# Linear attention and a two-layer FFN on one core: the low part of a decoded weight chunk is subtracted on VectorE instead of GpSimd

## The chip, the cores and the metric

One core of a Trainium2 chip runs the whole program. The metric is device time in microseconds. The core has TensorE (PE) for matrix products, VectorE (DVE), ScalarE (ACT) and GpSimd (POOL) for elementwise work, and SyncE (SP), which issues the transfers here. Each engine runs its own list of instructions in order.

## The reference

Eight batches, eight heads, 576 positions, 64 values a head. Linear attention with a normed output feeds a low-rank mixing over positions and a two-layer FFN of width 512 to 2048 to 512:

```python
kv = np.einsum('bhsd,bhse->bhde', k, v)
out = np.einsum('bhsd,bhde->bhse', q, kv)
rms = np.sqrt(np.mean(out * out, axis=-1, keepdims=True) + 1e-06)
x = out / rms * g_norm            # then heads side by side: [8, 576, 512]
...
h = x.transpose(0, 2, 1) @ U @ V
u = x + h.transpose(0, 2, 1)
ch = np.maximum(u @ w_ch1, 0.0) @ w_ch2
return (u + ch)
```

U, V and the two FFN weights arrive as 64-bit floating-point numbers, so the kernel receives their bits as 64-bit words and has to decode them itself.

## The kernel before

**Two parts for each number.** A product of full precision is made of three products of a shorter type (F32R): every operand is split into a high part, rounded by ScalarE, and a low part, the difference to it. FFN1 is thus high x high, high x low and low x high (lines 372 to 374), and FFN2 the same (line 389).

**The FFN.** The 4608 rows of u are cut into nine blocks of 512. For each block j, a loop runs over the 16 chunks f of the hidden width, 128 wide. `ffn1` makes 12 products into the one PSUM bank h (`ps_h`, one buffer). `relu` reads that bank twice: ScalarE writes the high part hh (line 381), then VectorE the low part hl (line 382); after that the bank can be filled again. `ffn2` adds the chunk before to four accumulators y, 12 products more. At the end of a block `finish` adds u in two steps, one on VectorE (line 400) and one on GpSimd (line 401), and writes the block out.

**The weights.** All 16 chunks stay in SBUF once they are decoded. Chunk 0 is decoded in the startup by a path of its own. Chunks 1 to 15 are decoded inside block 0, at most two chunks ahead (`AHEAD`) of the loop. One chunk is 128 partitions x 1024 words, w1 and w2 side by side. `decode_w` takes these steps:

- ScalarE's abs of the upper 32-bit half (line 82) into a temporary `dec`, of which there are two buffers;
- four VectorE operations on `dec`: clamp (line 85), shift and mask (86), merge the sign (88), merge the low bits (90);
- `split`: ScalarE copies `dec` into the high part (line 95), then an engine that is passed in subtracts it from `dec` and writes the low part (line 96). The buffer of `dec` is free after that.

The raw chunk and the finished one share their place in SBUF (`weight_slot`).

**The attention work.** While block j runs, the attention of batch j+1 is done in small steps between the FFN's: for each of four pairs of heads, the kv product (line 219), the output product (240, 242), its norm (243 to 267, of which 253 is a sum over 640 values and 255 to 258 are tiny operations on 128x10), a transposition (293) with 32 small transfers into `ut` (296), a split (103, 115, 281), the product with U (304, 313) and with V (364, 366), and the split of u (329, 330). In block 0 these steps stand closer together than later (`STEPS0`). In the startup the same work is done for batch 0 by lines 290 to 357, with line 348 as the split of u.

**What sets the order.** The program text gives a rough order, by the table `PLAN` in the startup and by the numbers of `STEPS0` and `STEPS` later. From that a scheduler lays out each engine's list when the kernel is built, by its own costs of the operations; so the lists move when an operation goes from one engine to another.

Of the kernel before, what the change touches and what calls it, by code (L numbers as in the profile page):

```python
# [47 lines left out]
def build(ctx: ExitStack, tc: tile.TileContext, kv_in, kvt0_in, kvt_in, q_in, uv_in, g_in, w_in, out):  # L48
    nc = tc.nc
# [22 lines left out]
    def weight_slot(name, shape, dtype, f):  # L72

        return const.tile(shape, dtype, name=name, tag=f"w_{f}")

    def decode(raw, tmp, n=None):

        words = raw.bitcast(U32).rearrange("p (n t) -> p n t", t=2)
        low, high = words[:, :, 0], words[:, :, 1]
        bits = tmp.bitcast(U32)  # L80
        if n is None or ENG["ab"][n] == "a":
            nc.scalar.activation(out=tmp, in_=high.bitcast(F32), func=AF.Abs)
        else:
            nc.vector.tensor_scalar(out=bits, in0=high, scalar1=0x7fffffff, scalar2=None, op0=ALU.bitwise_and)
        nc.vector.tensor_scalar(out=tmp, in0=tmp, scalar1=ABS_LO, scalar2=ABS_HI, op0=ALU.max, op1=ALU.min)  # L85
        nc.vector.tensor_scalar(out=bits, in0=bits, scalar1=3, scalar2=0x3fffffff,  # L86
                                op0=ALU.logical_shift_left, op1=ALU.bitwise_and)
        nc.vector.scalar_tensor_tensor(out=bits, in0=high, scalar=0xC0000000, in1=bits,  # L88
                                       op0=ALU.bitwise_and, op1=ALU.bitwise_or)
        nc.vector.scalar_tensor_tensor(out=bits, in0=low, scalar=29, in1=bits,  # L90
                                       op0=ALU.logical_shift_right, op1=ALU.bitwise_or)

    def split(hi, lo, src, lo_eng):

        nc.scalar.copy(out=hi, in_=src)  # L95
        lo_eng.tensor_tensor(out=lo, in0=src, in1=hi.bitcast(F32), op=ALU.subtract)  # L96
# [72 lines left out]
    def keep(which, f, hi, lo):  # L169
        w_sb[which][f] = [t.rearrange("p (d c) -> p d c", c=P) for t in (hi, lo)]  # L170
# [8 lines left out]
    def decode_w(f):  # L179

        tmp = dec.tile([P, 2 * DM], F32, name="dec")
        decode(raws.pop(f).rearrange("p w c -> p (w c)"), tmp)
        w = weight_slot(f"ws{f}", [P, 2, 2, DM], F32R, f)
        t = tmp.rearrange("p (w c) -> p w c", w=2)
        split(w[:, 0], w[:, 1], t, nc.gpsimd)
        for n, which in enumerate(("w1", "w2")):
            keep(which, f, w[:, 0, n], w[:, 1, n])

# [336 lines left out]
    for j in range(NBLK):  # L525
        todo = prep_schedule(j + 1)
        y = None
        for f in range(NF):
            if j == 0:
                while ahead < min(NF, f + 1 + AHEAD):  # L530
                    decode_w(ahead)
                    ahead += 1
            end = False
            if j == 0 and f < NEARLY:
                h = hs[f]
                ffn1(h, f, [3], j)
            else:
                end = j == NBLK - 1 and f == NF - 1
                h = ps_p.tile([P, BLK], F32, name="pp") if end else ps_h.tile([P, BLK], F32, name="h")
                ffn1(h, f, range(ND), j)  # L540
            hcur = (f, *relu(h, end))
            for w in todo.get(2 * f, []):
                w()
            if hprev is not None and not (j == NBLK - 1 and f > NF - 3):
                ffn2(y_prev if f == 0 else y, [hprev])
            if f == 0:
                if j > 0:
                    finish(y_prev, j - 1)
                y = outputs(j)
            for w in todo.get(2 * f + 1, []):  # L550
                w()
            held = (held + [hcur])[-3:]
            hprev = hcur
        y_prev = y
# [58 lines left out]
```

## Time and profile before

| | |
|---|---|
| time, median of 3 runs | 941.3 us (940.36 to 941.7) |
| the profiled execution | 941.2 us, span 939.4 us |
| mean granted TensorE clock | 0.993 of full speed |
| TensorE busy | 913.4 us, 97% of the span, 4550 products |
| VectorE busy | 428.2 us, 46%, 824 instructions |
| ScalarE busy | 237.6 us, 25% |
| GpSimd busy | 88.7 us, 9% |
| of it the 15 subtractions of line 96 on 128x1024 | 37.4 us, mean 2495 ns |

A row of a group gives line, engine, operation, the tile written and the tiles read, partitions x columns and type, the count, the busy time and the mean length. L96 is line 96 of the kernel. "PE h L372 <- DVE hl L382: 6.1, 4, 2.4" says that the TensorE product of line 372 into h waited 6.1 us in all, four times, at most 2.4 us, for the VectorE instruction of line 382 that wrote hl. In a timeline a row starts with its start and length in microseconds, counted from the start of the span; a bracket at its end is the idle time of the engine ahead of it, and what ended it. An instruction counts as busy from its start to its end, so time in which it stands inside is busy time too. The granted clock is 1.00 at full speed.

### The profile page before, as it was taken

What the parts mean: (1) busy time and instruction counts of PE and PEld (TensorE: products, weight loads), DVE (VectorE), ACT (ScalarE), POOL (GpSimd) and SP (SyncE); (2) the same over time, 40 slices, a digit from 0 to 9 for tenths busy, and PEclk for the clock granted to TensorE, in tenths of its full rate; (3) what the DMA queues carried; (4) which work ended last, traced back from release to release, by engine and by line L of the source; (5) the groups of instructions that cost most, each with busy time, mean ns of one, the idle gap of its engine ahead of it and who ended that gap; (6) DMA issues with size and microseconds to landing.
All of it is one profiled execution on the core that took longest, in us unless ns stands there. A gap on an engine that the chain in (4) does not pass through costs nothing.

```text
span 939.4 us, 11992 instructions
## 1 busy us (share of the span) xinstructions
PE 913.4 (97%) x4550; PEld 763.3 (81%) x4550; DVE 428.2 (46%) x824; ACT 237.6 (25%) x483; POOL 88.7 (9%) x82
## 2 busy tenths in 40 slices
PE   8789899999999999999999999999999999999998
PEld 7667678888888888888888888888788888888887
DVE  6999996445454344353354345334333331112112
ACT  5554442322222222222122222222222221111110
POOL 2333330100020002000110002000200020002000
PEclk9899999999999999999999999999999999999999
DMA  9951121321222112121122122212111010001001
GB/s 339 407 215 48 34 58 57 99 67 56 62 89 82 33 57 82 47 66 55 35 74 80 30 73 69 80 33 69 60 52 26 13 46 1 0 1 46 1 1 45
DMA packets 45034, 65.48 MB, mean 70 GB/s; under 512 B 9904, under 2 KB 28080, under 8 KB 44976
## 3 DMA queue, kind: packets, MB, share of 16 engines
q1 hardware_dynamic: 44976, 64.71, 21.2%
q8 instruction: 36, 0.59, 0.3%
q14 instruction: 22, 0.18, 0.1%
HBM read 46.97 MB, written 9.44 MB: 60 GB/s over the span
## 4 chain that ended last, share of the span: by engine, by line
PE 84%; DVE 13%; DMA 1%; issue 1%; SPq 0%; ACT 0%; POOL 0%; DVEq 0%; POOLq 0%
PE y L389 37%; PE h L372 13%; PE h L373 13%; PE h L374 13%; DVE dec L88 3%; PE pp L219 2%; PE pp L240 2%; DVE dec L90 2%; DVE dec L86 2%; PE pp L304 2%; DVE dec L85 1%; DVE hl L382 1%; DMA w1raw<-w_in 1%; PE pp L364 1%; PE pp L389 1%
## 5 line engine op out<-in xcount | busy, mean ns | idle before, releaser
L389 PE MATMUL y<-hh,ws 128*128 128x512 f32 (+1 forms) x1072 | 351.0, 394 | 0.1
L382 DVE SCALAR_TENSOR_TENSOR hl<-h,hh 128x512 fp32r<-128x512 f32 x142 | 97.8, 689 | 307.8 <-ACT hh L381 307.2
L389 PEld LDWEIGHTS y<-hh,ws 128*128 128x128 f32 x1072 | 194.3, 188 | 36.0 <-ACT hh L381 0.8
L372 PE MATMUL h<-uth,ws 128*128 128x512 f32 x536 | 212.5, 397 | 6.9 <-DVE hl L382 6.9
L373 PE MATMUL h<-utl,ws 128*128 128x512 f32 x536 | 210.1, 392 | 0.0
L374 PE MATMUL h<-uth,ws 128*128 128x512 f32 x536 | 209.9, 392 | 0.0
L389 PE MATMUL y<-hl,ws 128*128 128x512 f32 (+1 forms) x536 | 207.6, 387 | 0.0
L381 ACT ACTIVATE hh<-h 128x512 fp32r<-128x512 f32 x142 | 84.8, 597 | 409.2 <-PE h L374 409.1
L372 PEld LDWEIGHTS h<-uth,ws 128*128 128x128 f32 x536 | 101.4, 189 | 31.0 <-DVE hl L382 10.8
L374 PEld LDWEIGHTS h<-uth,ws 128*128 128x128 f32 x536 | 101.2, 189 | 21.9
L373 PEld LDWEIGHTS h<-utl,ws 128*128 128x128 f32 x536 | 101.4, 189 | 20.4
L389 PEld LDWEIGHTS y<-hl,ws 128*128 128x128 f32 x536 | 100.6, 188 | 20.5
L401 POOL TENSOR_TENSOR st<-st,utl 128x512 f32<-128x512 f32 x32 | 40.7, 1296 | 676.7 <-DVE st L400 673.6
L366 DVE TENSOR_TENSOR ut<-pp,ut 128x288 f32<-128x288 f32 x56 | 25.0, 456 | 53.6 <-DMA ut<-xt 39.0
L96 POOL TENSOR_TENSOR ws<-dec,ws 128x1024 fp32r<-128x1024 f32 x15 | 37.4, 2495 | 60.6 <-ACT ws L95 60.6
L400 DVE TENSOR_TENSOR st<-y,uth 128x512 f32<-128x512 f32 x32 | 21.2, 686 | 44.5 <-PE y L389 33.0
L329 ACT ACTIVATE uth<-ut,g_sb 128x448 fp32r<-128x448 f32 (+7 forms) x56 | 27.6, 530 | 48.0 <-DVE ut L366 33.6
L330 DVE SCALAR_TENSOR_TENSOR utl<-ut,g_sb,uth 128x448 fp32r<-128x448 f32 (+7 forms) x56 | 28.2, 534 | 14.7 <-ACT uth L329 10.9
L253 DVE TENSOR_REDUCE ss<-x 128x10 f32<-128x640 f32 x32 | 26.1, 814 | 19.0 <-ACT x L244 19.0
L219 PE MATMUL pp<-kv_sb 128*128 128x128 f32 x232 | 31.4, 275 | 0.5 <-DVE t L313 0.5
L219 PEld LDWEIGHTS pp<-kv_sb 128*128 128x128 f32 x232 | 29.3, 191 | 2.0 <-DVE t L313 0.9
L240 PE MATMUL pp<-kvb,q_sb 128*128 128x128 f32 x224 | 29.6, 274 | 0.0
(192 smaller groups left out, 754.8 us busy)
## 6 DMA issues: line engine op xcount, KB each, us to landing
raw<-w_in SPq DMA_DIRECT2D x30, 512.0 KB, 10.2
kv_sb<-kv_in SPq DMA_DIRECT2D x29, 512.0 KB, 3.5
q_sb<-q_in SPq DMA_DIRECT2D x29, 288.0 KB, 2.9
out<-st SPq DMA_DIRECT2D x32, 256.0 KB, 2.0
ut<-xt SPq DMA_DIRECT2D x224, 20.0 KB, 1.8
ut<-xt SPq DMA_DIRECT2D x224, 16.0 KB, 1.8
kvt_sb<-kvt_in SPq DMA_DIRECT2D x27, 128.0 KB, 3.2
kvq<-kv_in SPq DMA_DIRECT2D x3, 512.0 KB, 7.7
```

The source lines that it names most:

```text
L88: nc.vector.scalar_tensor_tensor(out=bits, in0=high, scalar=0xC0000000, in1=bits, op0=ALU.bitwise_and, op1=ALU.bitwise_or)
L96: lo_eng.tensor_tensor(out=lo, in0=src, in1=hi.bitcast(F32), op=ALU.subtract)
L219: nc.tensor.matmul(pp[:, 0:P], lhsT=m[:, i * P:(i + 1) * P], rhs=m[:, MAIN + i * P:MAIN + (i + 1) * P], start=(i == 0 and b < NATIVE), sto ...
L240: nc.tensor.matmul(big[:, i * P:(i + 1) * P], lhsT=qt[:, TAIL + i * P:TAIL + (i + 1) * P], rhs=kb, start=True, stop=True)
L330: nc.vector.scalar_tensor_tensor(out=lo, in0=src, scalar=g_sb, in1=hi.bitcast(F32), op0=ALU.mult, op1=ALU.subtract)
L372: nc.tensor.matmul(h, lhsT=w1s[f][0][:, d, :], rhs=uh[:, d, :], start=(d == 0), stop=False)
L373: nc.tensor.matmul(h, lhsT=w1s[f][0][:, d, :], rhs=ul[:, d, :], start=False, stop=False)
L374: nc.tensor.matmul(h, lhsT=w1s[f][1][:, d, :], rhs=uh[:, d, :], start=False, stop=(d == ND - 1))
L381: nc.scalar.activation(out=hh, in_=h, func=AF.Relu)
L382: nc.vector.scalar_tensor_tensor(out=hl, in0=h, scalar=0.0, in1=hh.bitcast(F32), op0=ALU.max, op1=ALU.subtract)
L389: nc.tensor.matmul(acc, lhsT=w2s[f][w][:, c, :], rhs=h[:, cols], start=(f == 0 and w == 0 and h is hh), stop=(f == NF - 1 and w == 1))
L401: nc.gpsimd.tensor_tensor(out=o, in0=o, in1=ul[:, c, :].bitcast(F32), op=ALU.add)
```

## The change

In `decode_w`, VectorE is passed to `split` instead of GpSimd:

```diff
         t = tmp.rearrange("p (w c) -> p w c", w=2)
-        split(w[:, 0], w[:, 1], t, nc.gpsimd)
+        split(w[:, 0], w[:, 1], t, nc.vector)
         for n, which in enumerate(("w1", "w2")):
```

`split` itself stays as it is. Fifteen instructions of line 96 go from GpSimd's list to VectorE's, and the lists of the other engines are laid out anew.

The first place is VectorE's list at the end of the startup, up to the first two low parts of the relu (hl, line 382). raw_151 and raw_162 are the raw words of the first two chunks decoded here, ws_515 and ws_524 the same chunks finished; raw_166 and raw_177 are the next two. Before:

```order
L90 SCALAR_TENSOR_TENSOR dec<-raw_162,dec 128x1024
L348 SCALAR_TENSOR_TENSOR utl<-y,g_sb,uth 128x512
L85 TENSOR_SCALAR dec<-dec 128x1024
L348 SCALAR_TENSOR_TENSOR utl<-pp,g_sb,uth 128x512
L86 TENSOR_SCALAR dec<-dec 128x1024
L88 SCALAR_TENSOR_TENSOR dec<-raw_166,dec 128x1024
L85 TENSOR_SCALAR dec<-dec 128x1024
L90 SCALAR_TENSOR_TENSOR dec<-raw_166,dec 128x1024
L86 TENSOR_SCALAR dec<-dec 128x1024
L382 SCALAR_TENSOR_TENSOR hl<-pp,hh 128x512
L382 SCALAR_TENSOR_TENSOR hl<-h,hh 128x512
```

The same place after the change:

```order
L90 SCALAR_TENSOR_TENSOR dec<-raw_162,dec 128x1024
L96 TENSOR_TENSOR ws_515<-dec,ws_515 128x1024
L348 SCALAR_TENSOR_TENSOR utl<-y,g_sb,uth 128x512
L96 TENSOR_TENSOR ws_524<-dec,ws_524 128x1024
L348 SCALAR_TENSOR_TENSOR utl<-pp,g_sb,uth 128x512
L85 TENSOR_SCALAR dec<-dec 128x1024 x2
L86 TENSOR_SCALAR dec<-dec 128x1024 x2
L88 SCALAR_TENSOR_TENSOR dec<-raw_166,dec 128x1024
L88 SCALAR_TENSOR_TENSOR dec<-raw_177,dec 128x1024
L382 SCALAR_TENSOR_TENSOR hl<-pp,hh 128x512
L382 SCALAR_TENSOR_TENSOR hl<-h,hh 128x512
```

Two subtractions have come in ahead of the second and the third L348, and the next two chunks go side by side through lines 85, 86 and 88 ahead of the first hl.

The second place is VectorE's list between the low part of the relu of the fourth chunk and that of the fifth (f = 3 and 4). Before:

```order
L382 SCALAR_TENSOR_TENSOR hl<-h,hh 128x512
L88 SCALAR_TENSOR_TENSOR dec<-raw_183,dec 128x1024
L90 SCALAR_TENSOR_TENSOR dec<-raw_183,dec 128x1024
L85 TENSOR_SCALAR dec<-dec 128x1024
L86 TENSOR_SCALAR dec<-dec 128x1024
L88 SCALAR_TENSOR_TENSOR dec<-raw_186,dec 128x1024
L382 SCALAR_TENSOR_TENSOR hl<-h,hh 128x512
```

The same place after the change, where ws_742 and ws_804 are the chunks of raw_180 and raw_183:

```order
L382 SCALAR_TENSOR_TENSOR hl<-h,hh 128x512
L96 TENSOR_TENSOR ws_742<-dec,ws_742 128x1024
L90 SCALAR_TENSOR_TENSOR dec<-raw_183,dec 128x1024
L85 TENSOR_SCALAR dec<-dec 128x1024
L86 TENSOR_SCALAR dec<-dec 128x1024
L96 TENSOR_TENSOR ws_804<-dec,ws_804 128x1024
L88 SCALAR_TENSOR_TENSOR dec<-raw_186,dec 128x1024
L382 SCALAR_TENSOR_TENSOR hl<-h,hh 128x512
```

Two subtractions have come in, and the L88 of raw_183 has moved ahead of the first hl. In GpSimd's list the 15 rows of line 96 on 128x1024 are gone, the four on 128x64 have stayed.

## The prediction

> **What bounds the kernel now.** The page comes first. Its 40 slices are 23.5 us each; VectorE (DVE) is full in slices 2 to 6 and less than half busy later, and the granted TensorE clock reads 9 or more from the third slice on.
>
> ```profile
> span 939.4 us, 11992 instructions
> ...
> DVE  6999996445454344353354345334333331112112
> ...
> PEclk9899999999999999999999999999999999999999
> ```
>
> Busy time by stretch, for core 0, says where the kernel is short of VectorE. The stretches from 53 to 141 us belong to the first FFN block, in which the weight chunks are decoded; the last one is the steady state behind it.
>
> ```profile
> core 0: us, PE busy (x) PEld busy (x) DVE busy (x) ACT busy (x) POOL busy (x), PEclk, DMA share, GB/s
> ...
> 53.00:70.00 17.00, 14.56 (x58) 11.58 (x57) 16.96 (x21) 7.80 (x9) 7.39 (x3) 0.90 0.40 153
> ...
> 84.00:100.00 16.00, 15.47 (x81) 12.41 (x81) 15.77 (x16) 8.16 (x14) 4.79 (x2) 1.00 0.20 60
> 100.00:120.00 20.00, 15.79 (x71) 11.98 (x69) 19.90 (x25) 8.85 (x14) 7.49 (x3) 0.91 0.18 46
> 120.00:141.00 21.00, 20.36 (x103) 16.65 (x104) 19.35 (x24) 8.89 (x15) 7.63 (x3) 1.00 0.21 60
> 141.00:200.00 59.00, 59.00 (x307) 49.82 (x306) 32.23 (x77) 16.95 (x39) 5.17 (x4) 1.00 0.26 80
> ```
>
> Up to 141 us VectorE has no free time (16.96 of 17 us, 19.90 of 20 us) and TensorE has gaps; from 141 us on TensorE is full (59.00 of 59 us) and VectorE is about half busy. So only time taken out of VectorE before 141 us can shorten the run, and only as far as TensorE stands still there. How far that is, TensorE's own waits in 38 to 142 us say (engine and line, what it waited for, total, times, longest); these are the four largest:
>
> ```profile
> PE h L372 <- DVE hl L382: 6.1, 4, 2.4
> PE pp L304 <- DVE xh L281: 1.7, 1, 1.7
> PE y L389 <- DVE hl L382: 1.2, 1, 1.2
> PE pp L242 <- DVE x L265: 1.1, 1, 1.1
> ```
>
> All are waits for VectorE, 10.1 us together. The next FFN1 product (L372) cannot start until hl (L382), the low half of the relu, has read the only h bank. After a wait the granted clock is down too: 0.90 over 17 us and 0.91 over 20 us, 1.7 + 1.8 = 3.5 us of TensorE time. These 10.1 + 3.5 = 13.6 us are about all that can be won.
>
> **What the moved instruction costs where it is.** GpSimd's (POOL) and VectorE's timelines, laid beside each other (start us, us, instruction):
>
> ```profile
> 58.37 2.50 POOL L96 TENSOR_TENSOR ws<-dec,ws 128x1024 fp32r<-128x1024 f32 x1 [3.51 <-ACT ws L95]
> ...
> 73.78 2.42 POOL L96 TENSOR_TENSOR ws<-dec,ws 128x1024 fp32r<-128x1024 f32 x1 [5.03 <-ACT ws L95]
> ```
>
> ```profile
> 58.53 2.37 DVE L258 SCALAR_TENSOR_TENSOR r<-ta,r 128x10 f32<-128x10 f32 x1
> ...
> 70.14 1.22 DVE L88 SCALAR_TENSOR_TENSOR dec<-raw,dec 128x1024 uint32<-128x1024 uint32 x1
> ...
> 73.98 3.30 DVE L88 SCALAR_TENSOR_TENSOR dec<-raw,dec 128x1024 uint32<-128x1024 uint32 x1
> 77.20 0.68 DVE L382 SCALAR_TENSOR_TENSOR hl<-h,hh 128x512 fp32r<-128x512 f32 x1
> 77.80 1.21 DVE L90 SCALAR_TENSOR_TENSOR dec<-raw,dec 128x1024 uint32<-128x1024 uint32 x1
> 78.94 0.68 DVE L85 TENSOR_SCALAR dec<-dec 128x1024 f32<-128x1024 f32 x1
> ...
> 121.62 0.16 DVE L258 SCALAR_TENSOR_TENSOR r<-ta,r 128x10 f32<-128x10 f32 x1
> ...
> 139.68 0.68 DVE L382 SCALAR_TENSOR_TENSOR hl<-h,hh 128x512 fp32r<-128x512 f32 x1
> ```
>
> L258 on 128x10 values takes 0.16 us at 121.62 and 2.37 us at 58.53, where it starts 0.16 us after a GpSimd subtraction and ends 0.03 us after it. L88 starts 0.20 us after the next one shown, and lasts 3.30 us: the rest of the subtraction, then its own length. So VectorE stands still, and is counted busy, while GpSimd subtracts. VectorE's "full" slices hold a large part of standing.
>
> How much, is in the groups of VectorE in 38 to 141 us (count | busy us, mean ns) against the medians of the same operations over the whole run (minimum/median/maximum):
>
> ```profile
> L88 DVE SCALAR_TENSOR_TENSOR dec<-raw,dec 128x1024 uint32<-128x1024 uint32 x14 | 27.7, 1980 | 0.2
> L90 DVE SCALAR_TENSOR_TENSOR dec<-raw,dec 128x1024 uint32<-128x1024 uint32 x14 | 19.0, 1355 | 0.1
> L86 DVE TENSOR_SCALAR dec<-dec 128x1024 uint32<-128x1024 uint32 x13 | 16.6, 1278 | 0.2
> L85 DVE TENSOR_SCALAR dec<-dec 128x1024 f32<-128x1024 f32 x13 | 10.1, 779 | 1.5 <-ACT dec L82 1.5
> ...
> L281 DVE TENSOR_TENSOR xh<-x,xh 64x128 fp32r<-64x128 f32 x3 | 3.0, 988 | 0.1
> L258 DVE SCALAR_TENSOR_TENSOR r<-ta,r 128x10 f32<-128x10 f32 x3 | 2.7, 895 | 0.0
> ...
> L330 DVE SCALAR_TENSOR_TENSOR utl<-ut,g_sb,uth 128x448 fp32r<-128x448 f32 x1 | 1.9, 1876 | 1.5 <-ACT uth L329 1.5
> ```
>
> ```profile
> L85 DVE TENSOR_SCALAR dec<-dec x15: 640/684/1971, 29.5 to 129.2; 128x1024 f32<-128x1024 f32 x15
> L86 DVE TENSOR_SCALAR dec<-dec x15: 677/694/2906, 30.2 to 130.1; 128x1024 uint32<-128x1024 uint32 x15
> L88 DVE SCALAR_TENSOR_TENSOR dec<-raw,dec x15: 1212/1225/3322, 33.4 to 132.7; 128x1024 uint32<-128x1024 uint32 x15
> L90 DVE SCALAR_TENSOR_TENSOR dec<-raw,dec x15: 1198/1217/3185, 36.4 to 134.4; 128x1024 uint32<-128x1024 uint32 x15
> L95 ACT CAST ws<-dec x15: 1041/1053/1058, 38.4 to 135.7; 128x1024 fp32r<-128x1024 f32 x15
> L96 POOL TENSOR_TENSOR ws<-dec,ws x15: 2357/2416/3026, 39.5 to 136.9; 128x1024 fp32r<-128x1024 f32 x15
> ```
>
> ```profile
> L281 DVE TENSOR_TENSOR xh<-x,xh x30: 284/285/2394, 17.9 to 733.8; 64x128 fp32r<-64x128 f32 x30
> ```
>
> Above the undisturbed length stand: L88 14 x (1.980 - 1.225) = 10.6 us, L90 14 x (1.355 - 1.217) = 1.9, L86 13 x (1.278 - 0.694) = 7.6, L85 13 x (0.779 - 0.684) = 1.2, L281 3 x (0.988 - 0.285) = 2.1, L258 3 x (0.895 - 0.16) = 2.2, and about 1.3 for the one L330 (I put its undisturbed length at 0.5 to 0.6 us, by L382's 0.68 us for 512 columns). Together 26.9 us, or 1.8 us for each of the 15 subtractions.
>
> **The change, part by part.** *Removed:* 15 GpSimd subtractions of 2.42 us. GpSimd itself bounds nothing; what leaves the path is the 26.9 us that VectorE stood. The four small subtractions of the first block and the 32 of the output (L401) stay on GpSimd, so standing in later blocks stays as it is, under a full TensorE.
>
> *Added:* 15 subtractions of 128x1024 on VectorE, a form that the trace does not show. The nearest rows are L88 and L90: the same size, two operands out of SBUF, one result into it. Their duration is 1.22 us, but L90 at 77.80 is followed by the next start at 78.94, 1.14 us later, as ends overlap starts. Bounds: 0.68 us each, the single-operand L85 of that size (10.2 us for 15), and 2.42 us each, GpSimd's own (36.2 us). I take 1.14 us, since L90 has every operand alike: 15 x 1.14 = 17.1 us. [...]
>
> *Waits added:* each subtraction needs the high part, ScalarE's L95 of 1.05 us, which needs L90. Were it queued right behind its own L90, VectorE would stand for 1.05 us and a little hand-over, with hl and everything TensorE wants queued behind. The new order does not do that: between chunk raw_183's L90 and its subtraction ws_804 stand L85 and L86, 0.68 + 0.69 = 1.4 us, and ahead of ws_524 another chunk's subtraction and L348. I read the tightest places as 0 to 0.5 us late, three or so in all, some 1 us. Against it stands VectorE's idle 1.5 us ahead of one L85, which waited for the abs of L82, which waited for the decode buffer that the slow subtraction held; a subtraction done in 1.14 us gives it back sooner. But at that place L85 comes twice in a row in the new order, and waits for two L82. I set these at nothing together, with 1.5 us either way.
>
> *Moved:* with GpSimd's rows gone, the scheduler has placed others anew. Between the hl of f = 3 and that of f = 4, VectorE now has L96, L90, L85, L86, L96, L88 and hl: 4 x 1.14 + 0.68 + 0.69 + 0.6 = 6.5 us. Before, the trace ran L88 from 70.14 to the end of hl at 77.80, 7.7 us. That is one interval of the eleven between f = 1 and f = 12, and a gain of 1.2 us in it. On SyncE some loads now stand ahead of the copies of x into ut; in the order five or more hl stand between that x and the first reader of its ut, so I cost this at nothing. If that slack were gone, a step would wait for one more load, whose median from issue to landing the page gives last in its row:
>
> ```profile
> kv_sb<-kv_in SPq DMA_DIRECT2D x29, 512.0 KB, 3.5
> ```
>
> **Sum.** VectorE: -26.9 + 17.1 + 0 = -9.8 us. TensorE had 13.6 us to give, so it can follow. The profiled execution took 941.2 us (span 939.4 and 1.8 around it), which is 0.1 us under the median of 941.3; 941.2 - 9.8 = 931.4 us. What is late next is VectorE still in the intervals with a batch of attention work, TensorE in the others.
>
> **Rivals.**
>
> *Half comes through (0.13).* The savings come evenly, the waits do not. In 84 to 100 us and 120 to 141 us TensorE was already busy 15.47 of 16 and 20.36 of 21 us. Six subtractions fall there or at their edges; each returns 1.8 - 1.14 = 0.66 us that TensorE cannot use: 4.0 us lost, 935.4 us; with 1.22 us for each new subtraction, 936.6. Against it: what VectorE gains there it carries forward as a lead to the next wait.
>
> *TensorE's floor (0.05).* All four waits and both clock dips go: 941.2 - 13.6 = 927.6 us or a little less. It takes a VectorE subtraction nearer to 0.68 than to 1.14 us, or an order that hides all bursts.
>
> *Slower: each subtraction waits for its own L95 (0.05).* VectorE is one queue; a subtraction at its head holds up hl, and hl the h bank. If all 15 waited out 1.05 us and some 0.15 us of hand-over, each would cost 1.14 + 1.2 = 2.34 us, 35.1 in all, and the run 941.2 - 26.9 + 35.1 = 949.4 us. It decides from a mean wait of 1.8 - 1.14 = 0.66 us each, where the gain is gone. For it: ScalarE is one queue as well, and L95 may stand behind a relu (L381) that waits for TensorE. Against it: the order puts other work in between.
>
> *Slower: the standing is not GpSimd's doing (0.02).* Then the 26.9 us stay and 17.1 come on top; the end would be 958.3 us, less what TensorE's slack took. The rows of L258 (0.16 and 2.37 us) speak clearly against it. [...]
>
> *No change (0.03).* VectorE's lead is eaten by later bursts in the same block. That the change does nothing can be left out: the order shows all 15 rows on VectorE and none on GpSimd.
>
> **Numbers.** About 0.2%, 1.9 us, is what a measurement of this kernel can tell from no change. The forecast, 931.4 us, has 0.72; its own spread is 927.6 to 934. With the half-gain case up to 936.6 the range holds 0.85, and the ends are TensorE's floor and the half-gain at the higher price. Faster: 0.72 + 0.13 + 0.05 = 0.90; same 0.03; slower 0.05 + 0.02 = 0.07.
>
> **What would show it.** In the changed profile L88, L86, L281 and L258 should have maxima near their medians in 38 to 141 us, L96 on VectorE should take 1.2 us with the next start 1.14 us on, VectorE should idle less than 2 us in total ahead of L96, TensorE's waits there should fall from 10.1 us to 3 or less, and the hl of f = 12 (it starts at 139.68 us before) should come near 130. The forecast is wrong if L88 keeps its 2 us mean, if VectorE idles 10 us for L95, or if TensorE's waits only change their names.

## The result

The changed kernel takes 935.04 us (median of 4 runs, 933.52 to 936.67), the kernel before 941.5 us beside it on the same chip (4 runs, 940.36 to 941.95). The ratio is 0.9933, with a 95% interval of 0.9909 to 0.9958: faster by 0.4 to 0.9%. The profiled execution is the shortest of the four, 933.52 us with a span of 931.7 us, 7.7 us shorter than the span of before.

The page of the changed kernel has the same shape as before with one difference: GpSimd (POOL) has next to nothing to do in the slices in which the weights are decoded. The single row below is GpSimd's of before.

```profile
span 931.7 us, 11988 instructions
...
DVE  6999987443453345444244435434344331112112
...
POOL 2100002000020002000200001000200020002000
```

```profile
POOL 2333330100020002000110002000200020002000
```

VectorE is full in slices 2 to 5 now, where it was full in slices 2 to 6. The groups of VectorE in 38 to 141 us say what has become of the standing (count | busy us, mean ns | idle ahead of them):

```profile
L96 DVE TENSOR_TENSOR ws<-dec,ws 128x1024 fp32r<-128x1024 f32 x15 | 18.2, 1216 | 0.7 <-ACT ws L95 0.7
L90 DVE SCALAR_TENSOR_TENSOR dec<-raw,dec 128x1024 uint32<-128x1024 uint32 x14 | 17.1, 1223 | 0.0
L88 DVE SCALAR_TENSOR_TENSOR dec<-raw,dec 128x1024 uint32<-128x1024 uint32 x14 | 17.1, 1226 | 0.1
...
L85 DVE TENSOR_SCALAR dec<-dec 128x1024 f32<-128x1024 f32 x13 | 9.0, 689 | 1.3 <-ACT dec L82 1.2
L86 DVE TENSOR_SCALAR dec<-dec 128x1024 uint32<-128x1024 uint32 x13 | 8.8, 682 | 0.1
...
L281 DVE TENSOR_TENSOR xh<-x,xh 64x128 fp32r<-64x128 f32 x4 | 1.1, 286 | 0.1
...
L258 DVE SCALAR_TENSOR_TENSOR r<-ta,r 128x10 f32<-128x10 f32 x4 | 0.7, 165 | 0.0
```

Every mean is now the undisturbed length: L88 1226 ns, where it was 1980; L86 682, where it was 1278; L258 165, where it was 895. The 15 subtractions have a busy time of 18.2 us, and VectorE idled 0.7 us in all for their high parts. VectorE's timeline shows how they follow one another, and how early the stage now ends:

```profile
67.21 1.22 DVE L96 TENSOR_TENSOR ws<-dec,ws 128x1024 fp32r<-128x1024 f32 x1
68.34 1.22 DVE L90 SCALAR_TENSOR_TENSOR dec<-raw,dec 128x1024 uint32<-128x1024 uint32 x1
...
71.01 1.22 DVE L96 TENSOR_TENSOR ws<-dec,ws 128x1024 fp32r<-128x1024 f32 x1
72.14 1.22 DVE L88 SCALAR_TENSOR_TENSOR dec<-raw,dec 128x1024 uint32<-128x1024 uint32 x1
73.28 0.68 DVE L382 SCALAR_TENSOR_TENSOR hl<-h,hh 128x512 fp32r<-128x512 f32 x1
73.88 0.68 DVE L85 TENSOR_SCALAR dec<-dec 128x1024 f32<-128x1024 f32 x1
...
126.41 0.69 DVE L382 SCALAR_TENSOR_TENSOR hl<-h,hh 128x512 fp32r<-128x512 f32 x1
...
143.21 0.69 DVE L382 SCALAR_TENSOR_TENSOR hl<-h,hh 128x512 fp32r<-128x512 f32 x1 [2.43 <-ACT hh L381]
```

A subtraction lasts 1.22 us, and the next operation starts 1.13 us after the subtraction's own start. The hl of f = 12 starts at 126.41 us, 13.3 us earlier than before. The last row is the hl of f = 15; that of before is here:

```profile
156.60 0.69 DVE L382 SCALAR_TENSOR_TENSOR hl<-h,hh 128x512 fp32r<-128x512 f32 x1 [2.84 <-ACT hh L381]
```

So at the end of the first block the changed kernel leads by 13.4 us, and the whole span is only 7.7 us shorter. The windows show where the rest stays (us, then TensorE's busy time):

```profile
84.00:100.00 16.00, 16.00 (x82) 13.32 (x81) 15.86 (x26) 7.79 (x14) 0.00 (x0) 1.00 0.18 56
100.00:120.00 20.00, 20.00 (x100) 16.56 (x98) 19.57 (x30) 9.88 (x15) 0.00 (x0) 1.00 0.18 50
120.00:141.00 21.00, 21.00 (x107) 17.66 (x106) 16.50 (x29) 8.31 (x16) 0.00 (x0) 1.00 0.15 38
141.00:200.00 59.00, 54.89 (x294) 46.08 (x293) 31.56 (x72) 15.88 (x37) 5.08 (x4) 1.00 0.28 82
```

From 84 to 141 us TensorE is full. Behind that, where it had been busy 59.00 of 59 us, it is now busy 54.89: 4.1 us of gaps that were not there before. TensorE's waits name them, first those in 38 to 142 us, then all later ones:

```profile
PE pp L372 <- DVE utl L348: 2.3, 1, 2.3
PE h L372 <- DVE hl L382: 1.9, 1, 1.9
PE y L389 <- DVE hl L382: 0.2, 1, 0.2
```

```profile
PE pp L219 <- DMA kv_sb<-kv_in: 2.6, 1, 2.6
PE pp L240 <- DVE kvb L230: 1.4, 1, 1.4
PE h L372 <- DVE hl L382: 0.8, 2, 0.4
```

From 38 to 142 us the waits were 11.1 us before (10.1 us in the four largest, which the prediction shows) and are 4.4 us now. Of these, 2.3 us stand ahead of the first hl, behind a split of u in the startup (L348); e_out_act below, with the same list of TensorE, has 0.2 us there. The last row of the second view, 0.8 us, was there before. The 2.6 and 1.4 us are new. They lie between 151 and 158 us, where block 1 begins and TensorE's list has attention work between the first FFN products: L240 needs the reduced kv product of batch 2 (`kvb`, line 230), L219 the next load of kv.

### The profile page after: what moved, and what is told of

The parts are those of the page before. It is cut to its first block, busy times and chain, and to the rows that moved or that the text cites. A ratio compares the mean times of both kernels' runs of the same rounds, so it can differ in the third digit from the quotient of the medians.

```text
span 931.7 us, 11988 instructions
## 1 busy us (share of the span) xinstructions
PE 910.7 (98%) x4550; PEld 763.4 (82%) x4550; DVE 418.4 (45%) x839; ACT 236.6 (25%) x483; POOL 49.9 (5%) x67
## 4 chain that ended last, share of the span: by engine, by line
PE 89%; DMA 6%; DVE 3%; SPq 0%; issue 0%; POOL 0%; DVEq 0%; POOLq 0%
PE y L389 40%; PE h L372 14%; PE h L373 13%; PE h L374 13%; DMA raw<-w_in 4%; PE pp L219 3%; PE pp L240 2%; PE pp L304 2%; DMA w2raw<-w_in 1%; PE pp L364 1%; PE pp L389 1%; PE pp L242 1%; DVE st L400 1%; DVE hl L382 1%; DVE dec L88 0%; DMA out<-st 0%
## 5 line engine op out<-in xcount | busy, mean ns | idle before, releaser
L400 DVE TENSOR_TENSOR st<-y,uth 128x512 f32<-128x512 f32 x32 | 21.2, 686 | 43.8 <-PE y L389 31.1
L219 PE MATMUL pp<-kv_sb 128*128 128x128 f32 x232 | 31.7, 275 | 2.6 <-DMA kv_sb<-kv_in 2.6
L330 DVE SCALAR_TENSOR_TENSOR utl<-ut,g_sb,uth 128x448 fp32r<-128x448 f32 (+7 forms) x56 | 27.0, 514 | 15.4 <-ACT uth L329 8.0
L219 PEld LDWEIGHTS pp<-kv_sb 128*128 128x128 f32 x232 | 29.7, 191 | 4.2 <-DMA kv_sb<-kv_in 3.1
L240 PE MATMUL pp<-kvb,q_sb 128*128 128x128 f32 x224 | 29.6, 275 | 1.4 <-DVE kvb L230 1.4
L240 PEld LDWEIGHTS pp<-kvb,q_sb 128*128 128x128 f32 x224 | 28.1, 191 | 2.4 <-DVE kvb L230 1.7
## 6 DMA issues: line engine op xcount, KB each, us to landing
raw<-w_in SPq DMA_DIRECT2D x30, 512.0 KB, 10.2
```

The costliest lines, as they stand in the source:

```text
L219: nc.tensor.matmul(pp[:, 0:P], lhsT=m[:, i * P:(i + 1) * P], rhs=m[:, MAIN + i * P:MAIN + (i + 1) * P], start=(i == 0 and b < NATIVE), sto ...
L240: nc.tensor.matmul(big[:, i * P:(i + 1) * P], lhsT=qt[:, TAIL + i * P:TAIL + (i + 1) * P], rhs=kb, start=True, stop=True)
L330: nc.vector.scalar_tensor_tensor(out=lo, in0=src, scalar=g_sb, in1=hi.bitcast(F32), op0=ALU.mult, op1=ALU.subtract)
L400: nc.vector.tensor_tensor(out=o, in0=acc, in1=uh[:, c, :].bitcast(F32), op=ALU.add)
```

## The experiments

Ten kernels were run. In a table of all of them, "lead" is by how much a given hl starts earlier than in the profile of before, and "end" the difference of the spans (939.4 us before):

| kernel | time, us | ratio to before (95%) | lead at the first hl | lead at f = 15 | end |
|---|---|---|---|---|---|
| the change | 935.04 | 0.9933 (0.9909 to 0.9958) | 1.0 | 13.4 | 7.7 |
| a_pool_too | 960.81, one run | | -0.3 | -21.3 | -19.6 |
| b_no_sub | 928.57, one run | | -1.0 | 13.8 | 12.6 |
| e_out_act | 934.41 | 0.9918 (0.9901 to 0.9935) | -1.7 | 11.9 | 6.2 |
| i_no_load | 934.58 | 0.9909 (0.9891 to 0.9928) | 0.4 | 12.7 | 5.6 |
| k_xt_act | 933.35 | 0.9911 (0.9896 to 0.9926) | -0.4 | 8.2 | 6.4 |
| l_mix9 | 932.03 | 0.9893 (0.9876 to 0.9909) | -0.3 | 8.8 | 9.2 |
| e_kv2 | 928.40 | 0.9855 (0.9840 to 0.9871) | -0.2 | 11.0 | 12.5 |
| f_before_kv2 | 943.79 | 1.0022 (1.0011 to 1.0033) | -2.2 | -6.1 | -4.6 |
| g_half_kv2 | 934.48 | 0.9918 (0.9900 to 0.9937) | 1.5 | 7.2 | 7.2 |
| h_twice_kv2 | 943.49 | 1.0016 (1.0005 to 1.0026) | 0.6 | -4.7 | -0.5 |

### Was the standing GpSimd's doing?

a_pool_too is the changed kernel, with GpSimd subtracting once more, behind VectorE, into the temporary, which nobody reads after that:

```diff
         split(w[:, 0], w[:, 1], t, nc.vector)
+        nc.gpsimd.tensor_tensor(out=t, in0=t, in1=w[:, 0].bitcast(F32), op=ALU.subtract)
```

> The changed kernel, and GpSimd does the subtraction once more behind VectorE's, into the temporary that nobody reads any more. If VectorE stands while GpSimd subtracts: VectorE's operations of the decode are stretched again, some 27 us in all on top of the 18 us of its own subtractions, and the run takes 950 to 960 us. If the standing is not GpSimd's doing: VectorE's operations keep their undisturbed lengths (L88 near 1.22 us in the mean), and the run stays at the 933 to 937 us of the changed kernel.

It took 960.81 us, 0.8 us above the range expected. Groups of VectorE in 38 to 141 us (lines behind the edit have moved by one, so L282 is L281):

```profile
L90 DVE SCALAR_TENSOR_TENSOR dec<-raw,dec 128x1024 uint32<-128x1024 uint32 x12 | 19.3, 1608 | 0.1
L96 DVE TENSOR_TENSOR ws<-dec,ws 128x1024 fp32r<-128x1024 f32 x12 | 16.4, 1362 | 0.0
...
L282 DVE TENSOR_TENSOR xh<-x,xh 64x128 fp32r<-64x128 f32 x3 | 7.0, 2343 | 0.1
```

The standing is back, on several of the operations that meet the subtraction: 2343 ns for an operation of 286. With it VectorE carries both prices, and the run is 19 us longer than before. The added subtraction also holds the temporary longer, but VectorE idled only 1.1 us ahead of L85 there, against 1.3 us in the changed kernel, so that is not where the time went. The rival in which the standing had another cause is dead. The three rows shown read two operands from SBUF. Two operands are not needed for it, though: in the kernel before, one L85 and four L86, which read one operand, lasted 1.97 to 2.91 us, and each of them started while a subtraction of GpSimd was running. And not every operation stands: in a_pool_too the hl at 77.82 us, which reads one operand from PSUM, started 0.91 us into a subtraction and lasted 0.69 us, where that at 139.68 us of the kernel before, with no subtraction beside it, took 0.68; the ten hl of 38 to 141 us have a mean of 686 ns. L115, with two operands from SBUF, started 0.10 us into a subtraction at 65.82 us of the kernel before and 0.39 us into one at 68.17 us of a_pool_too, and kept its 0.67 us; there the subtraction took longer, 3.03 and 3.26 us. What decides which of the two is held up is not shown.

### How much was there to win?

b_no_sub leaves the low part out: ScalarE rounds the high part as before and writes zeros in place of the low part, so no engine subtracts.

```diff
-        split(w[:, 0], w[:, 1], t, nc.vector)
+        nc.scalar.copy(out=w[:, 0], in_=t)
+        nc.scalar.mul(out=w[:, 1], in_=t, mul=0.0)
```

> The low part of chunks 1 to 15 is not computed at all: ScalarE writes zeros in its place, 15 more ScalarE copies of about 1.05 us. VectorE then has neither GpSimd's 27 us nor its own 18 us. If VectorE's time bounds the decode stage until TensorE's floor is reached: VectorE idles there, TensorE's waits for it go, and the run is at that floor, 925 to 930 us, or up to 4 us later if the block boundary takes its part as it does in the changed kernel. If the changed kernel is at TensorE's floor already: 933 to 935 us.

It took 928.57 us, and one wait of TensorE is left in 38 to 142 us (lines have moved by one here too):

```profile
PE y L390 <- ACT hh L382: 1.0, 1, 1.0
```

So about 928.5 us is TensorE's floor here, by one run, and the changed kernel stands 6.5 us above it.

### What holds the first block boundary?

The first idea was the DMA queue: kv's load stood on SyncE among block 0's stores. e_out_act has ScalarE issue these:

```diff
-            nc.sync.dma_start(out=out[j, c][:, cols], in_=o)
+            (nc.scalar if j == 0 else nc.sync).dma_start(out=out[j, c][:, cols], in_=o)
```

> The changed kernel with the four output transfers of the first block issued by ScalarE instead of SyncE; the lists of TensorE, VectorE and GpSimd are the same word for word. If the give-back at the first block boundary comes from kv_sb's load standing in SyncE's list behind output transfers that wait for GpSimd: the load starts as soon as its buffer is free, TensorE's wait of 2.6 us for it goes, and the run gains 2 to 3 us on the changed kernel (930 to 933 us). If the lead at the end of the decode stage was only work put off, so that TensorE would be behind at the boundary anyway: no change.

It took 934.41 us, and TensorE's waits behind 142 us were the same:

```profile
PE pp L219 <- DMA kv_sb<-kv_in: 2.6, 1, 2.6
PE pp L240 <- DVE kvb L230: 1.3, 1, 1.3
```

The stores do not hold the load up; that idea fell. The next took the load itself away: in i_no_load the kv product of batch 2, pair 1 reads pair 0's kv again, so that this pair's own kv is left out.

```diff
-            kt = ldp.tile([P, 2 * MAIN], F32, name="kv_sb")
-        nc.sync.dma_start(out=kt, in_=kv_in[b, p])
+            kt = loads["again"] = loads["again"] if (b, p) == (2, 1) else ldp.tile([P, 2 * MAIN], F32, name="kv_sb")
+        (b, p) != (2, 1) and nc.sync.dma_start(out=kt, in_=kv_in[b, p])
```

> The changed kernel without one load: the kv product of batch 2, pair 1, uses the kv_sb of pair 0 again (that batch's second pair is left wrong), so nothing waits for a load there. The lists are those of the changed kernel but for these four products, which stand two FFN products earlier. If the give-back at the first block boundary is the wait for the single kv_sb buffer: TensorE's 2.6 us for kv_sb are gone, the lead over the kernel before stays 2.6 us or more higher behind the boundary (10 to 11 us in place of 7.7), and the run takes 930 to 933 us. If the lists alone are to blame (two pairs' products among the FFN's): the lead falls to 7 to 8 us again, 933 to 937 us.

It took 934.58 us. TensorE's waits behind 142 us:

```profile
PE h L372 <- DVE hl L382: 2.0, 3, 1.2
PE pp L240 <- DVE kvb L230: 1.4, 1, 1.4
PE y L389 <- ACT hh L381: 1.1, 1, 1.1
```

The wait for the load is gone, and in its place stand 1.1 us for the relu and 1.2 us more for hl. The products concerned also stand two FFN products earlier in TensorE's list here. A wait that changes its name when its releaser is taken away was not the cause by itself; what is late, for a TensorE that comes 13 us earlier, this run does not show.

e_kv2 gives kv's tile a second buffer. That changes more than the load: the scheduler lays the lists out anew.

```diff
-            kt = ldp.tile([P, 2 * MAIN], F32, name="kv_sb")
+            kt = ldp.tile([P, 2 * MAIN], F32, name="kv_sb", bufs=2)
```

> The changed kernel with two buffers for kv_sb, so that a load need not wait for the products of the pair before; the scheduler lays the lists out anew. If the give-back is a late kv_sb: no wait of TensorE for kv_sb at the boundary, and 2 to 4 us less than the changed kernel, 929 to 932 us. If the lead was only work put off: 933 to 937 us as the changed kernel.

It took 928.4 us, 0.6 us below the range expected and at TensorE's floor; that is 13.3 us less than the kernel before beside it (941.73 us). The window behind the stage is full again:

```profile
141.00:200.00 59.00, 59.00 (x310) 49.87 (x310) 31.60 (x73) 15.41 (x35) 5.59 (x4) 1.00 0.30 90
```

Whether that is the buffer or the order, f_before_kv2 asks: the kernel before with the same edit.

> The kernel before, subtraction on GpSimd, with two buffers for kv_sb and nothing else. Behind the decode stage its lists are those of the run with both changes. If the second buffer only takes away a wait at the block boundary that the kernel before does not have: 940 to 942.5 us, no change, and the subtraction's own worth is the whole distance to the run with both, 12 to 14 us. If the second buffer is the gain in itself: 933 to 937 us.

It took 943.79 us, 0.1 to 0.3% longer than before and 1.3 us above the range in which the buffer wins nothing. The buffer by itself wins nothing. From the last chunks on, the lists of f_before_kv2 and e_kv2 are the same, and between their two profiles the lead is 17.1 us at f = 14 and 17.1 us for each hl of the rest of the block and of the next ones; 2.0 us of it came in the startup. Nothing is given back there. By the medians the subtraction's move is worth 943.79 - 928.4 = 15.4 us between these two kernels, where it was 6.5 us in the change as made.

Two last kernels went for the boundary itself. There the last quarter of block 1's u passes through sixteen copies (line 296) on SyncE, 10.0 us from the first to the end of the last, behind the transposition L293. k_xt_act has ScalarE issue eight of the sixteen:

```diff
-                    nc.sync.dma_start(out=ut32[p][32 * k:32 * k + 32, QO[a]:QO[a] + QL[a]],
+                    (nc.scalar if (b, p, a % 2) == (1, 3, 1) else nc.sync).dma_start(out=ut32[p][32 * k:32 * k + 32, QO[a]:QO[a] + QL[a]],
```

> The changed kernel; of the 16 copies that carry the last quarter of batch 1's attention result from the exchange (ut32[3]), the eight with odd a are issued by ScalarE's queue instead of SyncE's. In the changed kernel SyncE issued the sixteen one after the other, 10.0 us from the first to the last landing, and block 1's first product with that quarter came at 154.6 us. Theory (behind the decode stage TensorE waits, through a list of other work, for batch 1's attention chain): the copies take 5 to 6 us, L364 of pair 3 and the last L330 come 4 to 5 us earlier, the lead over the kernel before does not fall from 13 to 7.5 us at the first block boundary but to 10 to 13, and the run takes 929 to 932 us. Rival (what is lost there is the order of TensorE's list and its DMA loads, the chain is not late): L330 comes earlier, the lead still falls to 6 to 8, and the run takes 933 to 937 us.

It took 933.35 us. SyncE's part of the copies took half as long (first row below), and the two waits at the boundary went; but TensorE's timeline ahead of it shows others:

```profile
134.89 4.95 SPq L296 DMA_DIRECT2D ut<-xt  x8
```

```profile
141.11 0.53 PE L364 MATMUL pp<-v,t 128*128 128x288 f32 x2 [1.15 <-DVE t L313]
141.97 1.20 PE L389 MATMUL y<-hh,ws 128*128 128x512 f32 x4 [0.33 <-ACT hh L381]
143.17 0.62 PE L372 MATMUL h<-uth,ws 128*128 128x512 f32 x1
143.59 0.63 PE L373 MATMUL h<-utl,ws 128*128 128x512 f32 x1
...
146.92 0.39 PE L372 MATMUL h<-uth,ws 128*128 128x512 f32 x1
147.15 0.40 PE L373 MATMUL h<-utl,ws 128*128 128x512 f32 x1
```

The lists had moved with the edit, and the attention's products stand earlier in TensorE's; it waited 1.15 and 0.33 us among them, and its products then followed each other 0.42 us apart instead of 0.23. The time lies in the rival's range and 1.35 us above the theory's, and the lead of 8.0 us behind the boundary is the rival's too; but since the lists moved, the run does not decide between them. l_mix9 leaves the copies alone and changes one number of the due times, so that the attention's last product with V comes earlier in the lists:

```diff
-STEPS0 = dict(kv=1, out=2, t=6, mix=11, gap=3)
+STEPS0 = dict(kv=1, out=2, t=6, mix=9, gap=3)
```

> The changed kernel with one number of the list of due times of block 0 changed, mix=11 to mix=9: the attention's last mixing product (L364 of pair 3) and what hangs on it stand earlier in TensorE's, VectorE's and SyncE's lists, 29 instructions of TensorE's list ahead of block 1's first FFN product; no instruction is added or removed. Theory (attention chain of batch 1 is late at the first block boundary): TensorE has FFN work to do while the chain runs, the lead over the kernel before stays at 11 to 13 us behind the boundary, and the run takes 928 to 932 us. Rival (the loss is not the chain's): the lead falls to 6 to 8 us as in the changed kernel, and the run takes 933 to 937 us; if the earlier place makes TensorE wait for the copies inside the decode stage, that wait is seen at L364 in 130 to 145 us and the run takes 935 to 940 us.

It took 932.03 us, 1.1% less than before (0.9 to 1.2%), 0.03 us above the theory's upper end. The window behind the stage is full, and TensorE's waits behind 142 us are these:

```profile
141.00:200.00 59.00, 59.00 (x309) 50.08 (x308) 31.98 (x73) 15.80 (x36) 5.59 (x4) 1.00 0.29 90
```

```profile
PE y L389 <- DVE st L400: 0.8, 1, 0.8
PE h L372 <- DVE hl L382: 0.8, 2, 0.4
```

Both waits of the boundary are gone with no instruction added or removed; inside the stage, TensorE's waits for hl rose from 1.9 to 3.7 us. The lead is 8.8 us at f = 15 with more of the attention's work already done, 10.2 to 10.5 us for a long stretch behind it, and 9.2 us at the end: the 0.8 us for L400 comes at a later block's end. That is less than the 11 to 13 us of the theory and more than the 6 to 8 us of the rival. So the waits at the boundary belong to the order of the lists there. Which costs of the scheduler put the attention's steps too late in the change as made was not tried.

### Does VectorE still set the stage's length?

Both kernels stand on e_kv2, where nothing is given back. In g_half_kv2 VectorE subtracts the eight odd chunks alone, GpSimd the seven others:

```diff
-        split(w[:, 0], w[:, 1], t, nc.vector)
+        split(w[:, 0], w[:, 1], t, nc.vector if f % 2 else nc.gpsimd)
```

> Both changes, but only the odd chunks (8 of 15) subtract on VectorE; the even ones stay on GpSimd. If each subtraction that moves gives back the same standing, VectorE's time being the bound all through the stage: about 8/15 of the distance, 933 to 936 us. If TensorE's floor cuts the gain off early: 929 to 931 us, nearly all of it.

It took 934.48 us: 9.3 of the 15.4 us, or 60%, for 8 of 15 subtractions (53%). In h_twice_kv2 VectorE does each subtraction twice:

```diff
         split(w[:, 0], w[:, 1], t, nc.vector)
+        nc.vector.tensor_tensor(out=w[:, 1], in0=t, in1=w[:, 0].bitcast(F32), op=ALU.subtract)
```

> Both changes, and VectorE does each of the 15 subtractions twice, the second into the same place with the same values: 15 x 1.14 = 17.1 us more for VectorE. If VectorE still bounds the decode stage after the change: 14 to 17 us more than with one subtraction, 942 to 946 us, about where the kernel before stands. If TensorE bounds it by now and VectorE has room: 929 to 936 us.

It took 943.49 us. Groups of VectorE in 38 to 150 us, in which L186 is the second subtraction:

```profile
L96 DVE TENSOR_TENSOR ws<-dec,ws 128x1024 fp32r<-128x1024 f32 x14 | 17.2, 1226 | 0.1
...
L186 DVE TENSOR_TENSOR ws<-dec,ws 128x1024 fp32r<-128x1024 f32 x14 | 17.0, 1217 | 0.1
```

Fifteen more of 1.14 us are 17.1 us, and the run is 943.49 - 928.4 = 15.1 us longer: nearly all of VectorE's added time reaches the end. (2.0 us of TensorE's waits in 38 to 142 us are there for the second subtraction itself.) The moved work is paid nearly in full; it wins because the standing that it replaces was longer, 26.9 us by the prediction's count.

## Why the prediction was right, and where it was not

**The bound and the standing: right.** VectorE set the length of the decode stage (doubling its subtractions costs 15.1 us for 17.1 us of work), and the time above the undisturbed lengths was GpSimd's doing: it went with GpSimd's subtractions (L88 from 1980 to 1226 ns) and came back with them in a_pool_too (L282 at 2343 ns for 286). One reading was too strong: from 120 to 141 us VectorE was not without free time before, but busy 19.35 of 21 us.

**The price of the moved instruction: right.** L96 on VectorE lasts 1.22 us, and the next start is 1.13 us on, where 1.14 us was taken from L90. Its length is that of L88 and L90, and the next start comes 0.09 us ahead of its end (0.07 us for L90 at 77.80 us before).

**The waits for the high part: right.** They were set at nothing together with the idle time that goes; VectorE idled 0.7 us for L95, and the idle time for L82 went from 1.5 to 1.2 us. The interval from f = 3 to f = 4, from the start of L96 at 67.21 us to the next start behind hl at 73.88 us, took 6.7 us where 6.5 us was forecast.

**The sum for the stage: a little short.** It said 9.8 us. The lead at f = 15 is 13.4 us; 1.0 us of it is there at the first hl already, in a startup that varies by more than that from profile to profile (last section). Ahead of f = 15's last FFN1 product the changed list also holds nine products of L304 and two of L364 fewer than the list of before. They stand there from 150.59 to 151.45 us before and from 143.24 to 144.10 us now, so 0.9 us were put off. What is left is 13.4 - 1.0 - 0.9 = 11.5 us. Where the extra 1.7 us came from was not tried; L90 and L96 of the last chunk, 2.3 us, stand behind the hl of f = 12, where VectorE has idle time, while the sum charged all 15 subtractions to the path.

**The lists that moved: wrong, and this is why the run took 935.0 and not 931.4 us.** The prediction read the places where a load now stands ahead of the copies into ut, counted five or more hl of slack, and costed the move at nothing, and named the 3.5 us of one load as the price if that slack were gone. It was gone, though at another place: at the first block boundary TensorE, 13 us earlier, waited 2.6 us for a kv load and 1.4 us for L230, 4.0 us that were not there before. Of the 12.5 us that the lead is worth at f = 15 (13.4 less the 0.9 us put off), 7.7 are left, a loss of 4.8: these 4.0 us and 0.8 us that were not traced. i_no_load shows that the load alone is not the cause, l_mix9 that with the same instructions in another order these waits are gone; in e_kv2, with another order and a second buffer, they are gone too. Which instruction of the list is the late one stays open. The slack had been counted inside the stage, on lists that were laid out for a slower one, and not at its end.

**The range and the signs: partly luck.** The forecast's own spread ended at 934 us; 935.0 us lies in the range only through the half-gain case, whose reason did not come true. The upper end is a little off as well: at 1.22 us each, the length of L88 and L90, a subtraction returns 1.8 - 1.22 = 0.58 us, six of them 3.5 us and not 4.0, which gives 936.1 us where 936.6 stands. Two signs failed: TensorE's waits in the stage were to fall to 3 us or less and are 4.4 us, and behind the stage waits came up under new names.

**The rivals.** The half-gain case named 935.4 us, within half a microsecond of the median, but not its reason: it had six subtractions in 84 to 141 us return time that TensorE could not use. There TensorE went from 15.47 of 16 and 15.79 of 20 us to full, and the lead grew from 5.8 us at f = 7 to 13.3 at f = 10. The gain was carried forward, as the argument against it said, and lost behind the stage. TensorE's floor was put at 927.6 us; b_no_sub and e_kv2 have 928.6 and 928.4.

## What to carry to other kernels

Where an operation's mean is far above its minimum (here L88, 1980 against 1212 ns), ask what runs on the other engine at that moment: work moved onto the engine that is full can shorten it, if what it removes there is more standing than the work itself takes (26.9 us against 17.1 here). A faster stage runs into whatever was laid out for the slow one, so read the first stretch behind the stage, and its order, as closely as the stage; there a few microseconds were lost that one number of the due times won back. And when the wait that is named is taken away and another takes its place, look for the cause further back.

## What the hardware showed that was not expected

The startup differs from profile to profile although its lists are the same. Granted TensorE clock stands third from the end in these windows of the changed kernel, of e_out_act and of k_xt_act:

```profile
10.00:20.00 10.00, 8.69 (x71) 7.78 (x70) 9.56 (x25) 6.44 (x21) 4.36 (x11) 1.00 1.03 404
...
30.00:40.00 10.00, 6.17 (x45) 5.26 (x45) 9.81 (x19) 5.31 (x14) 1.37 (x3) 0.99 1.03 409
```

```profile
10.00:20.00 10.00, 9.09 (x47) 8.16 (x47) 8.10 (x18) 5.69 (x19) 4.66 (x12) 0.66 1.00 397
...
30.00:40.00 10.00, 8.60 (x47) 7.85 (x46) 9.43 (x22) 4.74 (x8) 0.61 (x1) 0.55 1.03 408
```

```profile
30.00:40.00 10.00, 8.23 (x34) 7.24 (x35) 9.73 (x17) 3.89 (x10) 0.95 (x2) 0.50 1.03 409
```

With 1.00 and 0.99 the first hl came 2.7 us earlier than with 0.66 and 0.55. Leads of a microsecond or two at the first hl are therefore not the change's.

The same clock also fell in the middle of a run, behind short waits: to 0.57 in 143 to 147 us of k_xt_act, after waits of 1.15 and 0.33 us, and to 0.57 in 160 to 164 us of i_no_load, after 1.1 and 1.2 us, each time about 1.7 us of TensorE's time. In the changed kernel the 1.4 us for L230 and the 2.6 us for kv's load were followed by full speed.

```profile
143.00:147.00 4.00, 3.99 (x11) 3.04 (x11) 1.45 (x4) 0.67 (x1) 0.00 (x0) 0.57 0.00 0
```

```profile
160.00:164.00 4.00, 3.77 (x10) 2.95 (x11) 3.48 (x10) 0.72 (x1) 0.00 (x0) 0.57 0.31 110
```

```profile
158.00:162.00 4.00, 4.00 (x22) 3.45 (x23) 3.77 (x12) 0.74 (x2) 0.00 (x0) 1.00 0.79 278
```

In these rows the granted clock was down to 0.50 to 0.66 in the startup and to 0.57 behind waits of little more than a microsecond, and it stood at 1.00 behind one of 2.6 us. What sets it off is not shown. In k_xt_act 1.5 us of waits came with 1.7 us more behind them (0.43 of 4 us), in i_no_load 2.3 us with as much, so these short waits of TensorE cost 2.1 and 1.7 times their length.
